# Where weight rounding, a batch's attention and its row shifts are placed at the head of an attention plus MLP kernel

## The chip, the cores and the metric

The kernel runs on one core of a Trainium2 chip. The metric is the device time of one execution in microseconds (us), as the median of several runs.

A core has five engines, each with its own list of instructions: TensorE (PE, matrix products), VectorE (DVE), ScalarE (ACT), GpSimd (POOL), and SyncE, whose queue (SPq) does nothing here but start transfers. In the traces of this case, an engine that waits holds up what stands behind in its list: in the changed kernel, a fold that TensorE needed stood on GpSimd behind an operation that waited 7.2 us for a transfer.

## The reference

```python
def reference(q, k, v, moe_w_ch1, moe_w_ch2):      # q, k, v: (8, 8, 576, 64) float32
    # attention inside chunks of 64 tokens, per batch and head
    scores = q_c @ k_c^T / sqrt(64);  attn = softmax(scores);  x = attn @ v_c   # -> (8, 576, 512)
    mixed = real(fft(fft(x, axis=1), axis=2))
    u  = x + mixed
    un = (u - mean(u)) / sqrt(var(u) + 1e-6)
    return u + relu(un @ w_ch1) @ w_ch2            # 512 -> 2048 -> 512
```

The weights arrive as 64-bit floats. The kernel turns them to 32 bits itself, with integer operations on their halves.

## The kernel before

The program is a list of steps that is written out once. Each batch has attention, a Fourier stage (products `z`, then `mix`) and an MLP (16 up steps, then down steps). The MLP of one batch is interleaved with the attention and the Fourier stage of the next. The weights come in 32 pieces of 128 x 512, and each is rounded by eight instructions on three engines. The line numbers in the traces of before (L246 and so on) are those of this code:

```python
def round_weight(i):                       # cut to its instructions
    if i < len(pieces):                    # first half of piece i
        nc.vector.tensor_scalar(wi, hi, 0x000FFFFF, None, ALU.bitwise_and)      # L244
        nc.scalar.activation(out=w, in_=wi, func=ACTF.Copy, ...)                # L245
        nc.vector.tensor_scalar(p, hi, 0x7FF00000, None, ALU.bitwise_and)       # L246
        nc.scalar.activation(out=p, in_=p, func=ACTF.Relu, ...)                 # L247, L248
    if 0 < i <= len(pieces):               # second half of piece i - 1
        nc.vector.scalar_tensor_tensor(w, lo, 2.0 ** -52, w, ALU.mult, ALU.add)             # L253
        nc.vector.scalar_tensor_tensor(p, hi, 0x80000000, p, ALU.bitwise_and, ALU.bitwise_or) # L254
        nc.gpsimd.tensor_tensor(out=w, in0=w, in1=p.bitcast(FP32), op=ALU.mult)             # L255
        ...                                # give the buffer back, start the next piece's load
```

The loop over the steps `t` of the MLPs places everything else. `conv2` combines the rounded second weight matrix into sums and differences on GpSimd (L592) and stores them for the later MLPs. It starts once rounding is through:

```python
for g in range(NG):
    for _ in mlp(g):
        t += 1
        round_next()                       # one rounding call
        if t % 2:
            round_next()                   # and a second one in every other step
        if n_w > len(pieces):              # all calls made:
            for _ in range(2):
                next(conv2, None)          # two parts of the weight combinations
        # ... other weight work cut ...
        if cur < len(sides):               # attention and Fourier stage of the next batch
            t0 = KF + 1 if cur == 0 else ready_at[cur - 1]      # KF = 16
            t1 = ready_at[cur]             # 26 for batch 1
            due = min(sizes[cur], (t - t0) * sizes[cur] // (t1 - t0))
            while done < due:
                next(sides[cur], None)
                done += 1
```

Between attention and Fourier stage stand `shift`, six small transfers that move rows by one, and `fold`, which adds and subtracts halves. For batch 1 the folds run on GpSimd.

Of the kernel before, what the change touches and what calls it, by code (L numbers as in the profile page):

```python
# [8 lines left out]
FP32 = mybir.dt.float32  # L9
U32 = mybir.dt.uint32  # L10
ACTF = mybir.ActivationFunctionType
ALU = mybir.AluOpType
# [4 lines left out]
def kernel(  # L17
# [29 lines left out]
    nc = tc.nc  # L47
# [10 lines left out]
    KF = DFF // 128  # L58
# [51 lines left out]
    tiles, first = [], []  # L110
# [22 lines left out]
    def kind(n):  # L133
        return tiles[n][0]
# [87 lines left out]
    def raw(i):  # L222
        r = raws[i]
        t = xall[:, r:r + 2, :].rearrange("p a f -> p (a f)")[:, 0:1024]
        return t.bitcast(U32).rearrange("p (f r) -> p f r", r=2)

    def load_weight(i):

        if i < len(pieces) and free and (i < N_EARLY or free[0] in RAWS[:3]):
            raws[i] = free.pop(0)  # L230
            nc.sync.dma_start(out=raw(i).rearrange("p f r -> p (f r)"), in_=pieces[i][1].bitcast(U32))

    def round_weight(i):






        if i < len(pieces):  # L240
            w, t = pieces[i][0], raw(i)
            lo, hi, wi = t[:, :, 0], t[:, :, 1], w.bitcast(U32)
            p = power[i] = three_p.tile([128, 512], U32, tag="o", name="power")
            nc.vector.tensor_scalar(wi, hi, 0x000FFFFF, None, ALU.bitwise_and)  # L244
            nc.scalar.activation(out=w, in_=wi, func=ACTF.Copy, scale=2.0 ** -20, bias=1.0)  # L245
            nc.vector.tensor_scalar(p, hi, 0x7FF00000, None, ALU.bitwise_and)  # L246
            nc.scalar.activation(out=p, in_=p, func=ACTF.Relu, scale=-1.0, bias=top[:, 0:1])  # L247
            nc.scalar.activation(out=p, in_=p, func=ACTF.Relu, scale=-8.0, bias=top[:, 1:2])  # L248
        if 0 < i <= len(pieces):
            w, t = pieces[i - 1][0], raw(i - 1)  # L250
            lo, hi = t[:, :, 0], t[:, :, 1]
            p = power.pop(i - 1)
            nc.vector.scalar_tensor_tensor(w, lo, 2.0 ** -52, w, ALU.mult, ALU.add)  # L253
            nc.vector.scalar_tensor_tensor(p, hi, 0x80000000, p, ALU.bitwise_and, ALU.bitwise_or)  # L254
            nc.gpsimd.tensor_tensor(out=w, in0=w, in1=p.bitcast(FP32), op=ALU.mult)  # L255
            r = raws.pop(i - 1)
            if i - 1 + len(RAWS) < N_EARLY or r in RAWS[:3]:
                free.append(r)
            load_weight(max(raws, default=i - 1) + 1)
# [9 lines left out]
    def att_T(n):  # L269

        a = qs.pop(n)
        pt = turn(lambda j: a[:, 2 * j:2 * j + 2, :].rearrange("p h d -> p (h d)"))
        t = one_p.tile([128, 2 * NJ, CH + 1], FP32, tag="qT", name="qT")
        low = kind(n) == LO
        nc.scalar.copy(t[:, :, CH:0:-1] if low else t[:, :, 0:CH], pt.rearrange("p j (c t) -> p (j c) t", c=2))
        if low:
            nc.gpsimd.tensor_copy(t[:, :, 0:1], t[:, :, CH:CH + 1])
        qT[n] = t
        a2 = ks.pop(n)
        pt = turn(lambda j: a2[:, 2 * j:2 * j + 2, :].rearrange("p h d -> p (h d)"))  # L280
        t = one_p.tile([128, NJ, 128], FP32, tag="kT", name="kT")
        nc.vector.tensor_copy(t, pt)
        kT[n] = t
        if first[1] <= n + 1 < NT:
            load(n + 1)
# [66 lines left out]
    def shift(b):  # L352

        lows = [xt(at[LO, b, i]) for i in range(NM)]
        r = b % 2 * CH
        rest = xt(rests[b // 2])[r:r + 1, 0:DM]
        eng = nc.gpsimd if b == 0 else nc.sync
        t = three_p.tile([128, XW], FP32, tag="y", name="first")
        for i in range(NM):
            eng.dma_start(out=t[2 * i:2 * i + 2, 0:DM], in_=lows[i][0:CH + 1:CH, 0:DM])  # L360
        eng.dma_start(out=t[2 * NM:2 * NM + 1, 0:DM], in_=rest)
        for i in range(NM):
            eng.dma_start(out=lows[i][0:CH + 1:CH, 0:DM], in_=t[2 * i + 1:2 * i + 3, 0:DM])
        eng.dma_start(out=rest, in_=t[0:1, 0:DM])
# [425 lines left out]
    with tc.manual_schedule():  # L790
        make_identity(nc, ident)
        nc.vector.memset(sign, -1.0)
        nc.vector.memset(sign[0:1, :], 1.0)
        nc.vector.memset(eps, 1e-6)
        nc.vector.memset(warm, 0.0)
        nc.vector.memset(top[:, 0:1], float((896 + 255) << 20))
        nc.vector.memset(top[:, 1:2], float(255 << 23))
        nc.scalar.preload_act_table_set("natural_log_exp_and_others")
        for n in range(3):
            load(n)  # L800
            load_v(n)
        load(3)
        load_tables()
        load_weight(0)
        load(4)
        load_weight(1)
        load_dim_tables()
        for i in range(2, len(RAWS)):
            load_weight(i)
        n_w = 0  # L810
        idle = ps_f.tile([128, 512], FP32, tag="ff", name="idle")

        def keep_warm(times):

            for _ in range(times):
                nc.tensor.matmul(out=idle[:, 0:NQ], lhsT=warm[:, 0:128], rhs=warm[:, 0:NQ], start=True, stop=True)  # L816

        def round_next():
            nonlocal n_w
            if n_w <= len(pieces):  # L820
                round_weight(n_w)
                n_w += 1

        for step, _ in enumerate(attention(0)):
            if step == 9:
                turn_tables()
            if step > 7 and step % 4 == 1:
                round_next()
            if step > 3:
                keep_warm(2)  # L830
        keep_warm(2)
        for step, _ in enumerate(fourier(0)):
            if step < 4:
                round_next()
            else:
                for s in range(2 * (step - 4), 2 * (step - 4) + 2):
                    normed(0, s)
        for s in range(G):
            keep_warm(6 if s % 2 == 0 else 0)
            turned(0, s)  # L840

        def side(b):
            yield from attention(b)
            yield from fourier(b)

        sides = [list_ for list_ in (side(b) for b in range(1, B))]
        sizes = []
        for b in range(1, B):
            n_tiles = first[b + 1] - first[b]
            sizes.append(4 * n_tiles + 4 + NM + b % 2)  # L850
        done, cur = 0, 0
        begin = [0]
        for g in range(NG):
            begin.append(begin[-1] + (KF if g < first_of[1] else 2 * HF) + (G * PARTS if g < first_of[2] else 2 * NO))
        ready_at = [begin[g] + (KF + G * PARTS - 6 if g < first_of[2] else 2 * HF + 4) for g in range(NG)]
        conv2 = iter([step for i in range(HF // 2) for step in [keep2(i)]])
        conv1 = iter([step for i in range(4) for step in [keep1(i)]])

        def chain(gens):
            for gen in gens:  # L860
                yield from gen

        conv2, conv1 = chain(conv2), chain(conv1)
        t = 0
        for g in range(NG):
            for _ in mlp(g):
                t += 1
                round_next()
                if t % 2:
                    round_next()  # L870
                if n_w > len(pieces):
                    for _ in range(2):
                        next(conv2, None)
                if t == begin[1] - 1:
                    for _ in conv2:
                        pass
                if begin[1] <= t < begin[1] + KF // 2:
                    for _ in range(3):
                        next(conv1, None)
                if t == begin[1] + KF // 2:  # L880
                    for _ in range(NS2):
                        fetch(2)
                if t == begin[1] + KF:
                    for _ in range(NS1):
                        fetch(1)
                if cur < len(sides):
                    t0 = KF + 1 if cur == 0 else ready_at[cur - 1]
                    t1 = ready_at[cur]
                    due = min(sizes[cur], (t - t0) * sizes[cur] // (t1 - t0))
                    while done < due:  # L890
                        next(sides[cur], None)
                        done += 1
                    if t >= t1:
                        for _ in sides[cur]:
                            pass
                        cur, done = cur + 1, 0
# [49 lines left out]
```

## Time and profile before

| | before |
|---|---|
| time, median (lowest to highest) | 1255.4 us (1251.8 to 1256.7) |
| span of the profiled run | 1251.5 us |
| first matmul of the first MLP | 81.3 us |
| last multiply of a weight piece starts | 160.5 us, on GpSimd |
| first score product of batch 1 starts | 166.9 us |
| first matmul of the second MLP | 272.4 us |
| from there to the end | 979.1 us |

The page gives an engine's busy share in 40 equal slices, in tenths. A PE digit under 9 is where time may be won. The stretches view, the chain of waits and the waits by engine are quoted in the prediction below. What to remember from them: PE stood 21.5 us before the first score product of batch 1 and 9.8 us before its first Fourier product. From 272 us to the end it was busy for 962 of 979 us.

### The profile page before, as it was taken

The numbers are of one execution on the slowest core, as the hardware profiler recorded it, in microseconds if no ns is written. First come the engines' busy times: TensorE is split into PE (matmuls) and PEld (weight loads), VectorE is DVE, ScalarE is ACT, GpSimd is POOL, SyncE is SP. The second block draws the span as 40 slices with busy tenths as digits, with TensorE's granted clock in tenths as the row PEclk, the third lists the DMA queues.
The fourth block names the chain that finished last, engine by engine and source line by source line (L and its number), as shares of the span: only waits on it lengthen the run. The fifth ranks groups of instructions, "written<-read, shape, count | busy, mean of one in ns | idle before, by whom it ended". The sixth has DMA issues, their size and how long they took to land.

```text
span 1251.5 us, 18517 instructions
## 1 busy us (share of the span) xinstructions
PE 1178.4 (94%) x7148; PEld 895.5 (72%) x7148; DVE 564.6 (45%) x1176; ACT 291.8 (23%) x645; POOL 308.0 (25%) x370
## 2 busy tenths in 40 slices
PE   7889666999999999999999999999999999999998
PEld 5554233444578777887788878877888788888887
DVE  4579842332334544455254535453445343423431
ACT  3347720112211321122212221122113211210310
POOL 0335445133430033102220314013402240130130
PEclk9899878999999999999999999999999999999999
DMA  9624547039524752575237524763364235445422
GB/s 196 159 93 155 166 126 208 23 102 308 155 96 144 213 147 76 158 216 158 80 140 210 170 76 135 201 179 111 125 187 129 81 122 195 155 135 182 138 70 99
DMA packets 175871, 182.11 MB, mean 146 GB/s; under 512 B 121574, under 2 KB 132327, under 8 KB 168615
## 3 DMA queue, kind: packets, MB, share of 16 engines
q1 hardware_dynamic: 173990, 180.51, 48.0%
q8 instruction: 57, 0.93, 0.3%
q10 hardware_dynamic: 1600, 0.39, 0.2%
q14 instruction: 32, 0.25, 0.1%
q0 software_dynamic: 192, 0.02, 0.0%
HBM read 156.60 MB, written 24.12 MB: 144 GB/s over the span
## 4 chain that ended last, share of the span: by engine, by line
PE 82%; DVE 9%; DMA 3%; ACT 2%; POOL 1%; SPq 1%; issue 1%; ACTq 0%; DVEq 0%; POOLq 0%
PE pb L737 18%; PE pb L690 15%; PE pa L737 14%; PE pa L690 11%; PE up L626 5%; PE pt L265 5%; PE z L442 4%; PE dn L645 3%; PE mix L485 3%; PE xp L332 2%; PE sc L294 2%; DVE power L246 1%; DMA xall<-in_moe_w_ch_dram 1%; PE idle L816 1%; DVE power L254 1%
## 5 line engine op out<-in xcount | busy, mean ns | idle before, releaser
L618 POOL TENSOR_TENSOR h<-h 128x256 f32<-128x256 f32 x64 | 56.8, 891 | 506.9 <-PE pb L690 323.4
L626 PE MATMUL up<-unT,wa 128*128 128x512 f32 x256 | 113.9, 597 | 1.8 <-ACT h L633 0.9
L737 PE MATMUL pa<-wb,h 128*128 128x256 f32 x512 | 115.6, 381 | 0.0
L737 PE MATMUL pb<-wb,h 128*128 128x256 f32 x512 | 115.1, 381 | 0.0
L690 PE MATMUL pb<-unT,wa 128*128 128x256 f32 x448 | 106.4, 380 | 8.6 <-DVE wa L699 8.6
L690 PE MATMUL pb<-wa 128*128 128x256 f32 x448 | 108.6, 385 | 1.1 <-DVE h L707 0.9
L690 PE MATMUL pa<-unT,wa 128*128 128x256 f32 x448 | 107.6, 383 | 0.0
L737 PEld LDWEIGHTS pa<-wb,h 128*128 128x128 f32 x512 | 95.8, 190 | 16.2 <-issue 3.8
L737 PEld LDWEIGHTS pb<-wb,h 128*128 128x128 f32 x512 | 95.6, 190 | 12.7
L690 PEld LDWEIGHTS pb<-unT,wa 128*128 128x128 f32 x448 | 84.5, 190 | 22.2 <-DVE wa L699 10.7
L690 PEld LDWEIGHTS pb<-wa 128*128 128x128 f32 x448 | 82.2, 190 | 16.2 <-issue 3.4
L690 PEld LDWEIGHTS pa<-unT,wa 128*128 128x128 f32 x448 | 82.5, 190 | 12.0 <-issue 1.2
L626 PEld LDWEIGHTS up<-unT,wa 128*128 128x128 f32 x256 | 47.2, 190 | 56.4 <-issue 52.0
L645 PE MATMUL dn<-wb,h 128*128 128x512 f32 x128 | 61.9, 630 | 0.0
L500 POOL TENSOR_TENSOR xall<-y,xall 128x513 f32<-128x513 f32 x16 | 27.6, 1723 | 128.9 <-DVE y L493 128.9
L737 PE MATMUL pa<-wb,yall 128*128 128x256 f32 x256 | 58.2, 381 | 0.0
L737 PE MATMUL pb<-wb,yall 128*128 128x256 f32 x256 | 57.9, 381 | 0.0
L737 PE MATMUL pb<-wb 128*128 128x256 f32 x256 | 56.6, 379 | 0.0
L690 PE MATMUL pa<-wa 128*128 128x256 f32 x224 | 53.4, 381 | 2.1 <-ACT wa L695 2.1
L697 DVE TENSOR_TENSOR wa<-pa,wa 128x256 f32<-128x256 f32 x56 | 23.8, 425 | 69.8 <-PE pa L690 69.7
L737 PEld LDWEIGHTS pa<-wb,yall 128*128 128x128 f32 x256 | 48.1, 190 | 8.6 <-issue 2.3
L737 PEld LDWEIGHTS pb<-wb 128*128 128x128 f32 x256 | 48.6, 190 | 6.6
(151 smaller groups left out, 1736.1 us busy)
## 6 DMA issues: line engine op xcount, KB each, us to landing
wb<-s SPq DMA_DIRECT2D x56, 1024.0 KB
wa<-s SPq DMA_DIRECT2D x196, 256.0 KB
xall<-in_moe_w_ch_dram SPq DMA_DIRECT2D x32, 512.0 KB
v<-in_v_dram SPq DMA_DIRECT2D x142, 64.0 KB
s<-yall SPq DMA_DIRECT2D x24, 256.0 KB
s<-wb SPq DMA_DIRECT2D x20, 256.0 KB
q<-in_q_dram SPq DMA_DIRECT2D x34, 128.0 KB
k<-in_k_dram SPq DMA_DIRECT2D x34, 128.0 KB
```

The costliest lines, as they stand in the source:

```text
L265: nc.tensor.transpose(pt[:, j, :], src(j), ident)
L294: nc.tensor.matmul(out=sc[t0:t0 + CH, e, j * CH:(j + 1) * CH], lhsT=a[r0:r0 + D, 2 * j + c, 0:CH], rhs=b[r0:r0 + D, j, t0:t0 + CH], start= ...
L332: nc.tensor.matmul(out=xp[t0:t0 + CH, e, j * D:(j + 1) * D], lhsT=a[r0:r0 + CH, j, t0:t0 + CH], rhs=b[r0:r0 + CH, c, j, :], start=True, st ...
L442: nc.tensor.matmul(out=z[:, 0:NQ], lhsT=pm[p, fold_, half], rhs=tk[p, i, fold_, :], start=(i == 0), stop=(i == NM), skip_group_check=(T == 2),
L485: nc.tensor.matmul(out=o[:, cols], lhsT=zt[:, T], rhs=tab, start=(T == 0), stop=(T == 3), skip_group_check=True,)
L500: eng.tensor_tensor(out=x[:, 0:w], in0=y[:, 0:w], in1=x[:, 0:w], op=ALU.add)
L618: nc.gpsimd.tensor_tensor(out=h1[:, m, hi], in0=h1[:, m, lo], in1=h1[:, m, hi], op=ALU.subtract)
L626: nc.tensor.matmul(out=up, lhsT=w1[:, kk, m * 128:(m + 1) * 128], rhs=unT[:, kk], start=(kk == 0), stop=(kk == KD - 1),)
L645: nc.tensor.matmul(out=dn, lhsT=h1[:, m, s * 128:(s + 1) * 128], rhs=w2[:, m, :], start=(m == 0), stop=(m == KF - 1),)
L690: nc.tensor.matmul(out=dst, lhsT=w[:, kk, r], rhs=rhs[o][:, kk], start=(o in (0, 2) and kk == 0), stop=(kk == 1), skip_group_check=True,)
L697: nc.vector.tensor_tensor(out=b, in0=dst, in1=a, op=ALU.add)
L737: nc.tensor.matmul(out=dst, lhsT=lhs[:, m], rhs=w[:, m], start=(o in (0, 2) and m == 0), stop=(m == HF - 1), skip_group_check=True,)
```

## The change

The intent is to fill these waits. The multiply L255 leaves GpSimd. Batch 1's attention is spread over 18 steps of the first MLP instead of 9. The key copies of batches 0 and 1 go to ScalarE and the row shifts of batch 1 to GpSimd's queue. Two smaller edits move rounding calls.

```diff
-            nc.gpsimd.tensor_tensor(out=w, in0=w, in1=p.bitcast(FP32), op=ALU.mult)
+            nc.vector.tensor_tensor(out=w, in0=w, in1=p.bitcast(FP32), op=ALU.mult)
@@ att_T: key copy
-        nc.vector.tensor_copy(t, pt)
+        if n < first[2]:
+            nc.scalar.copy(t, pt)
+        else:
+            nc.vector.tensor_copy(t, pt)
@@ shift
-        eng = nc.gpsimd if b == 0 else nc.sync
+        eng = nc.gpsimd if b < 2 else nc.sync
@@ first Fourier stage
-            if step < 4:
+            if step < 3:
                 round_next()
-            else:
+            elif step > 3:
                 ... normalise ...
@@ loop over the MLP steps
-                if t % 2:
+                if t % 2 == 0:
                     round_next()
@@
-                    t0 = KF + 1 if cur == 0 else ready_at[cur - 1]
+                    t0 = KF // 2 if cur == 0 else ready_at[cur - 1]
```

## The prediction

> **What bounds the kernel now.** I read the page first, for where TensorE (PE) is not full.
>
> ```profile
> PE   7889666999999999999999999999999999999998
> DVE  4579842332334544455254535453445343423431
> PEclk9899878999999999999999999999999999999999
> ```
>
> A digit is a tenth of a slice of 31.3 us. PE shows 9 (90% or more) from the eighth slice on, so the shortfall lies early. Next, the chain of waits: from 272.47 us, the second MLP's first matmul, it is almost only matmuls, so those 979 us are PE's own work, and the change leaves their program order alone. Everything must come from before 272. The stretches view splits the first MLP (us, busy time per engine with instruction counts, granted clock, DMA):
>
> ```profile
> 81.00:145.00 64.00, 62.78 (x150) 27.98 (x151) 57.86 (x85) 47.19 (x76) 30.65 (x20) 1.00 0.45 147
> 145.00:167.00 22.00, 0.45 (x8) 0.21 (x7) 14.50 (x20) 10.23 (x17) 13.03 (x11) 0.60 0.36 97
> 167.00:204.00 37.00, 34.70 (x354) 19.78 (x354) 16.40 (x30) 6.87 (x12) 13.80 (x17) 0.96 0.67 181
> 204.00:214.00 10.00, 0.22 (x1) 0.22 (x2) 0.07 (x1) 0.00 (x0) 4.51 (x9) 0.68 0.88 253
> 214.00:222.00 8.00, 8.00 (x12) 3.34 (x13) 0.19 (x1) 0.46 (x2) 4.10 (x5) 0.55 0.71 236
> ```
>
> Two holes: 145 to 167 and 204 to 214, the second followed by 8 us at about half clock. The waits by engine name their ends:
>
> ```profile
> PE sc L294 <- POOL qT L277: 21.5, 1, 21.5
> PE z L442 <- POOL pm L388: 9.8, 1, 9.8
> ```
>
> The first hole: up to 145 us PE ran ahead (16 up steps of 3.44 us, two down steps), then met the first score product of batch 1. That product needs copies of its queries and keys, which stand on ScalarE (ACT), VectorE (DVE) and GpSimd (POOL) behind the rounding of all 32 weight pieces; the last piece leaves POOL at 161.7, and four POOL subtractions of the first weight combination come before the query copy. The second: the Fourier product waits for a fold on POOL, which waits for row shifts and for stores on SyncE's backed-up queue. Why rounding lags, in order of time:
>
> ```profile
> 100.39 1.42 DVE power L246
> 101.81 0.60 DVE wa L253
> 102.41 0.64 DVE power L254
> ...
> 151.83 3.71 DMA xall<-in_moe_w_ch_dram
> 155.56 1.03 DVE wb L244
> 156.59 0.34 DVE power L246
> ```
>
> A piece costs DVE 0.34 + 1.42 + 0.60 + 0.60 = 2.96 us to about 127 us. L246 takes 0.34 us alone, but 1.42 whenever POOL's multiply (L255, median 1.386 us) runs beside it. After 127 us three buffers are left and two pieces take 6.2 us, half of that a transfer.
>
> **What the Trainium skill says.** "SBUF — State Buffer", section "SBUF: two separate sides": DVE and GpSimd share a port pair as an exclusive lock for a whole instruction. The trace agrees: 1.42 against 0.34 us. "GPSIMD Engine Reference", section "Engine selection": elementwise two-input work is about twice as slow on GpSimd. Agrees: 1.39 us against 0.60 to 0.68 for DVE's two-input L253. "TensorE: Matmul & The Clock Gate", section "Why this matters for your kernels": no PE gaps over about 3 us, or the clock halves. Agrees: 0.55 granted after the 9.8 us hole. "DMA: Bandwidth & Descriptors", section "Issuing engines are not separate DMA queues": another issuing engine saves only sequencer time. Here this is the point: SyncE issued without a break from 190.3 to 204 us at about 0.6 us each, with the shift in the middle at 195.9.
>
> **The change part by part.**
>
> Multiply on DVE: per piece DVE loses the 1.08 us blockage and gains a two-input instruction, which I put at L253's 0.60. New cost 0.34 + 0.34 + 3 x 0.60 = 2.48 us, 0.48 less. ACT needs about 1.9 us per piece (three instructions; starts at 85.50 and 87.39) plus 0.5 per up step. With 1.5 pieces per step DVE needs 3.72 us a step, ACT 3.35, PE 3.44: nearly level. POOL is free, so the query copy no longer stands behind anything.
>
> Head of the program: one rounding call fewer in the first Fourier stage. There the ACT chain of the last call (65.76 to 67.7) stood before the copy of the mix at 67.66, whose data needed only the evict that ended at 64.85 and a 0.5 us matmul. Worth about 2 us, and key copies on ACT take 0.56 us from in front of the first row shift (key copy 31.23, x write 31.79). I take 2.5 us for both. The call itself moves into the first MLP.
>
> Attention of batch 1 now starts after up step 8 instead of 16 and runs 23 parts over 18 steps instead of 9. Before, 2 parts were done when rounding ended; now 12. On PE the ten extra parts are 2.5 tiles of 2.55 us (queries and keys 0.87, scores 0.62, weights turned 0.44, values 0.62), 6.4 us that fall into the old hole. On DVE the same parts cost: four score groups of 2.5 us plus about 0.7 of waiting for the exponential, two value writes of 0.68, 14 us in all, now between pieces. So DVE from 81 to the last piece: 26 first halves x 0.68 + 27 second halves x 1.80 = 66.3, plus 14, plus about 4 us at the start (ACT is held by the first evict until PE ends an up step at 85.0, then the second) = 165.4 us. That is 4 us later than 161.7: the freed DVE time is spent on attention. I walked the steps on all four engines with these durations; PE waits about 6 us at its first score product (113 to 119), keeps DVE's pace, and ends its 19th step with the two attention parts behind it near 169 to 170 us.
>
> From there PE has 13 down steps x 3.44 = 44.7, two attention parts 1.1, Fourier and mix 15.1, turned activations 1.8, first parts of batch 2 4.0: 66.7 us. Before, the same reckoning from 167 gives 79.3 us of work against 105.5 elapsed, so 26 us of waits and slow clock.
>
> How much of this wait stays? The shift goes to POOL's own queue and ends, after the batch 1 value write near 159, by about 166 to 168 (three issues, a landing, three issues; batch 0's took 10 us). It is then off the path. But batch 1's last fold still stands on POOL behind the second weight combination, which waits for stores of the first: issue near 175, landing 5 us later as at 173.2 to 178.3, then 3 x 1.27 of subtractions and 2.4 of fold, so near 186.5. PE reaches its first Fourier product near 180.5: still a 6 us hole, plus about 4 us at half clock (before: 9.8 and 4). The end (mix, statistics, normalise, turn) keeps about 5 us of waits, a little less because the first mix is one step earlier. Sum: 169.5 + 66.7 + 6 + 4 + 5 = 251 for the start of the second MLP, against 272.5, and 248.5 with the 2.5 us of the head. **Gain 24 us**, and 1255 - 24 = 1231; I round to 1230, since nothing is counted for steps that run ahead.
>
> **The rivals.**
> (a) Lockstep. With attention among the pieces the four in-order engines wait for each other every step: ACT's up evict waits for PE, PE for ACT's query copy, DVE for PE's scores. For it: DVE and ACT are within 11% of each other per step, and a stalled PE falls to half clock. Against: PE has slack to 169 us either way. If it costs 1 us in each of the ten steps with attention, 1240.
> (b) Both holes close. If POOL's earlier start on combinations (free since about 167) and the free SyncE queue put the fold ahead of PE, the 6 + 4 us vanish: 1220. Against: the store wait occurred three times in the trace (20.5 us in total) and the order between fold and combination is unchanged.
> (c) Transfers stay the bound of rounding. 3.5 us to land against 3.1 us of DVE work between freeing and reuse in the three-buffer ring; with attention in between it is about 3.9, so transfers should be hidden. Were they not, the last piece would come at most 3 us later: 1233.
> (d) The gain is given back after 272. PE is at 9 tenths in every slice and keeps its order there, so no: time won before goes through to the end.
>
> **Range and chances.** Rivals (a) and (b) set the spread: 1219 to 1241. The 2% line is 1229.9, on my centre. Faster by over 2% 0.48, within 2% 0.51, slower 0.01: no part adds PE work, and PE now idles over 30 us before 272.
>
> **What would show it.** L246 at about 0.42 us throughout, the multiply on DVE at 0.6 to 0.7, GpSimd nearly idle from 81 to 155. The last piece at 160 to 168. The 21.5 us wait of PE for the query copy gone, in its place one of about 6 us near 115 and short ones to 160. A wait of the first Fourier product for the fold of 3 to 8 us, now near 182. The first mix copy near 65.5 instead of 67.66. First matmul of the second MLP near 248 instead of 272.5, and 979 us from there to the end. I am wrong in the mechanism if the last piece is past 172 or before 155, if the Fourier product waits for nothing, or if the stretch after the second MLP's start changes by over 3 us.

## The result, and the profile after

The changed kernel takes 1237.5 us in the median (1234.4 to 1239.9, four runs) against 1255.4 (four runs). The ratio is 0.986, with a 95% interval of 0.983 to 0.989. A ratio here is the mean time of one kernel's runs over that of the other's in the same rounds, so it is not quite the ratio of the medians. The gain is 17.9 us where 24 to 25 was expected. The profiled run was the fastest of the four, and its span (1232.6 us) is 18.9 us shorter than that of the profiled run before, so the two traces differ by 1 us more than the medians.

The same rows of the changed kernel's page (busy tenths in 40 slices of 30.8 us, granted clock):

```profile
PE   7798987999999999999999999999999999999998
DVE  3678860523244535455345444552545343523421
PEclk9898998999999999999999999999999999999999
```

The run of three 6s in PE has gone. What remains is an 8 in the fourth slice and an 8 and a 7 in the sixth and seventh. The stretches of the changed kernel, cut at its own waits (length, busy us and count of PE, weight loads, DVE, ACT and POOL, then clock, DMA share, GB/s):

```profile
78.00:142.00 64.00, 56.70 (x236) 27.03 (x237) 54.33 (x106) 47.81 (x79) 0.57 (x2) 0.95 0.55 156
142.00:165.00 23.00, 18.61 (x113) 9.41 (x111) 20.87 (x42) 16.99 (x28) 1.60 (x3) 0.93 0.70 174
165.00:184.00 19.00, 18.51 (x144) 9.21 (x142) 9.61 (x14) 2.50 (x5) 11.42 (x16) 1.00 0.60 142
184.00:192.00 8.00, 0.00 (x0) 0.00 (x0) 0.00 (x0) 0.00 (x0) 5.74 (x7) 0.68 0.72 230
192.00:200.00 8.00, 7.80 (x15) 3.57 (x16) 0.19 (x1) 0.46 (x2) 7.03 (x8) 0.68 0.25 88
```

The 22 us in which PE stood are filled: from 142 to 165 it works 18.6 of 23 us. DVE is now the fullest engine there (20.9 of 23). A stretch without any PE work remains from 184 to 192, the old second hole; the granted clock is 0.68 in it and in the 8 us after it. The waits of PE by engine (total us, times, longest us) name both that are left:

```profile
PE z L445 <- POOL pm L391: 8.7, 1, 8.7
PE sc L297 <- ACT kT L283: 6.0, 1, 6.0
```

Rounding in the changed kernel, from the chain of waits (start, us, engine, tile, line). It answers the three lines of 100 to 103 us in the prediction:

```profile
101.11 0.61 DVE power L254
...
101.74 0.69 DVE wa L255
102.43 0.34 DVE wa L244
102.77 0.34 DVE power L246
103.11 0.60 DVE wa L253
```

L246 takes 0.34 us instead of 1.42, with GpSimd idle. The multiply costs DVE 0.69 us. A piece is 0.34 + 0.34 + 0.60 + 0.63 + 0.69 = 2.60 us from start to start, against 2.96 before.

The second MLP starts at 253.6 us, and from there to the end it is 979.0 us as before. So only what lies before the second MLP changed: the first MLP starts at 78.3 us instead of 81.3, and takes 175.3 instead of 191.1.

The remaining hole in the chain of waits of the changed kernel, in order of time:

```profile
167.25 1.29 POOL yall L595
...
177.34 8.58 DMA s<-yall
...
186.05 1.26 POOL yall L595
...
187.39 2.48 POOL yall L595 x2
...
190.08 1.27 POOL sum L380
...
191.42 0.74 POOL pm L391
...
192.20 2.59 PE z L445 x4
```

Read from the bottom: the Fourier product waits for the fold (`pm`). The fold's sum stands on GpSimd behind three operations of the second weight combination (186.05 and 187.39). Those overwrite `yall` and so wait, 7.2 us, until the first combination's stores (`s<-yall`) have read it.

### The profile page after: what moved, and what is told of

It reads as the page before. It is cut to its first block, busy times and chain, and to the rows that moved or that the text cites. A ratio compares the mean times of both kernels' runs of the same rounds, so it can differ in the third digit from the quotient of the medians.

```text
span 1232.6 us, 18509 instructions
## 1 busy us (share of the span) xinstructions
PE 1176.6 (95%) x7148; PEld 893.8 (73%) x7148; DVE 560.2 (45%) x1199; ACT 296.0 (24%) x654; POOL 266.1 (22%) x344
## 4 chain that ended last, share of the span: by engine, by line
PE 82%; DVE 8%; DMA 3%; ACT 3%; POOL 2%; issue 1%; SPq 0%; POOLq 0%; ACTq 0%; DVEq 0%
PE pb L740 18%; PE pb L693 15%; PE pa L740 14%; PE pa L693 11%; PE up L629 6%; PE pt L265 4%; PE z L445 4%; PE mix L488 3%; PE xp L335 2%; PE dn L648 2%; PE sc L297 2%; PE idle L819 1%; PE z L455 1%; DVE ex L308 1%; DMA first<-xall 1%
## 5 line engine op out<-in xcount | busy, mean ns | idle before, releaser
L629 PE MATMUL up<-unT,wa 128*128 128x512 f32 x256 | 117.4, 607 | 0.9 <-DVE unT L537 0.9
L693 PEld LDWEIGHTS pb<-unT,wa 128*128 128x128 f32 x448 | 84.5, 190 | 22.2 <-DVE wa L702 10.7
## 6 DMA issues: line engine op xcount, KB each, us to landing
wa<-s SPq DMA_DIRECT2D x196, 256.0 KB
s<-yall SPq DMA_DIRECT2D x24, 256.0 KB
s<-wb SPq DMA_DIRECT2D x20, 256.0 KB
```

The source lines that it names most:

```text
L629: nc.tensor.matmul(out=up, lhsT=w1[:, kk, m * 128:(m + 1) * 128], rhs=unT[:, kk], start=(kk == 0), stop=(kk == KD - 1),)
L693: nc.tensor.matmul(out=dst, lhsT=w[:, kk, r], rhs=rhs[o][:, kk], start=(o in (0, 2) and kk == 0), stop=(kk == 1), skip_group_check=True,)
```

## The experiments

Three theories were on the table. Theory A: DVE's rounding chain sets when PE may go on, and the hole at the Fourier product is the fold queued behind the second combination. Rival B: the hole is the round trip of the row shift. Rival C: transfers, or the lockstep of four in-order engines, set the pace of rounding by now. All kernels gave correct results. All times are medians of four runs, ratios are to the kernel before in the same rounds, and the changed kernel is 0.986. The experiments ran on three chips, on which the kernel before took 1254.9 to 1257.1 us, so a difference of 2 us between two medians shows nothing.

### The multiply back on GpSimd (u_mult)

```diff
-            nc.vector.tensor_tensor(out=w, in0=w, in1=p.bitcast(FP32), op=ALU.mult)
+            nc.gpsimd.tensor_tensor(out=w, in0=w, in1=p.bitcast(FP32), op=ALU.mult)
```

> The changed kernel with the multiply of the weight pieces back on GpSimd, all else kept. Theory A (VectorE's rounding chain sets when PE may go on, and the port shared with GpSimd slows it): L246 goes back to 1.4-1.5 us, a piece costs VectorE 2.96 instead of 2.60 us, the last piece ends 7 to 10 us later than 168 us, second MLP starts near 262 instead of 253.6, time 1245 us (1242 to 1248). Rival C (transfers or the lockstep with PE and ScalarE set the pace of rounding by now): the slack takes it up, at most 2 us, 1237 to 1239.

Measured: 1239.2 us, ratio 0.987 (0.984 to 0.990). The second MLP starts at 256.5 us, 3 us later. Theory A's size is refuted, and the time is the one that rival C gave. L246 did go back to 1.4 us up to 134 us. Later the attention's instructions stand between the pieces and L246 takes 0.42 us in the records again. DVE then runs out of pieces instead, as its waits in this run show (us, times, longest):

```profile
DVE wb L244 <- DMA xall<-in_moe_w_ch_dram: 6.1, 5, 2.1
```

In the changed kernel the same wait is 1.4 us in total. DVE's last rounding instruction (L254) ends at 169.0 us, as the last multiply does in the changed kernel (169.1): without the multiply DVE has less to do for a piece, and late in the phase this pays for the early stretching and the waits. On GpSimd the last three multiplies stand behind the row shift, which waits 5.0 us for its own transfer. They run from 170.3 to 174.0, the first combination follows them, and the first Fourier product starts at 193.8 us instead of 192.2.

### The multiply alone, on the kernel before (a_mult)

```diff
-            nc.gpsimd.tensor_tensor(out=w, in0=w, in1=p.bitcast(FP32), op=ALU.mult)
+            nc.vector.tensor_tensor(out=w, in0=w, in1=p.bitcast(FP32), op=ALU.mult)
```

> The kernel before with only the multiply moved to VectorE. Theory A: the last piece ends 5 to 7 us before 161.7 and the query copy no longer queues behind multiplies and follows at once, so the 21.5 us wait shrinks to 13 to 16 us; the second wait stays; 1246 to 1250. Theory C1 (transfers in the three-buffer ring hide it): 1252 to 1256.

Measured: 1247.1 us, ratio 0.994 (0.992 to 0.996), as theory A expected. The last multiply starts at 156.7 us (it ends 4.3 us before 161.7, a little less than expected), and PE's first wait is 13.6 us instead of 21.5. The second grew to 11.7. So the same edit is worth about 8 us by itself and, inside the whole change, 1 to 2 us, which lies within the spread. It and the spread attention fill the same hole.

### Batch 1's attention from step 17 again (u_spread)

```diff
-                    t0 = KF // 2 if cur == 0 else ready_at[cur - 1]
+                    t0 = KF + 1 if cur == 0 else ready_at[cur - 1]
```

> The changed kernel with batch 1's attention started at step 17 again, all else kept. Theory A: rounding ends 12 to 14 us earlier (154 to 156 us), but PE idles until then and has the attention after it: second MLP starts at 258 to 262, time 1243 us (1240 to 1247). Rival C (lockstep between the four engines during the spread attention costs what the spread gains): 1237 us or less.

Measured: 1243.3 us, ratio 0.990 (0.986 to 0.993), as theory A expected. The last multiply starts at 156.9 us, PE waits 13.3 us for the keys of the first score product, and the second MLP starts at 263.5, some 2 us later than expected. Spreading the attention is worth some 5 us here, although it puts off the start of the last multiply by 10.

### Batch 1's row shift back on SyncE (u_shift)

```diff
-        eng = nc.gpsimd if b < 2 else nc.sync
+        eng = nc.gpsimd if b == 0 else nc.sync
```

> The changed kernel with batch 1's row shift back on SyncE's queue. Theory A (the hole before the Fourier product is the last fold queued on GpSimd behind the second combination, which waits for the first one's stores; these are issued after the output store at 175.65 us whoever issues the shift): the Fourier wait stays 7 to 10 us, time within 2 us of the changed kernel. Rival B (the shift's round trip sets the hole): the wait changes by 4 us or more, and the time with it; 1242 us or more if SyncE's queue is the worse place.

Measured: 1236.0 us, ratio 0.984 (0.982 to 0.987). The Fourier wait is 8.7 us, unchanged. In the profiled run, the slowest of the four, the second MLP starts at 256.0 us, 2.5 us later than in the changed kernel; the times don't show that. Rival B falls: the queue of the shift is worth nothing measurable here.

### The key copies back on VectorE (u_key)

```diff
-        if n < first[2]:
-            nc.scalar.copy(t, pt)
-        else:
-            nc.vector.tensor_copy(t, pt)
+        nc.vector.tensor_copy(t, pt)
```

> The changed kernel with the key copies of batches 0 and 1 back on VectorE. Theory A (VectorE is the engine that paces rounding and attention together): four copies of 0.6 to 0.7 us more on it before the last piece, and one in front of the first row shift; second MLP starts 2 to 4 us later (256 to 258), time 1240 us. Rival (ScalarE is loaded nearly as much, so either engine will do): 1236 to 1238.

Measured: 1238.5 us, ratio 0.985 (0.983 to 0.987). No difference is shown. The profiled run has its second MLP at 260.2 us, but it was the slowest of the four runs (1241.0, the fastest 1235.0), so this one trace doesn't decide for theory A.

### Batch 1's folds and second add on VectorE (n_fold2)

```diff
-        eng = nc.vector if b == 0 else nc.gpsimd                 # fold
+        eng = nc.vector if b < 2 else nc.gpsimd
+        sm = nc.vector if b == 1 else nc.gpsimd                  # used for the small copies and the clear
@@ normalisation add
-                eng = nc.gpsimd if kind(n) == HI else nc.vector
+                eng = nc.gpsimd if kind(n) == HI and b != 1 else nc.vector
```

> The changed kernel with batch 1's folds, the small copies and the clear beside them, and its second normalisation add on VectorE instead of GpSimd, so that nothing of batch 1's Fourier stage queues behind the weight combinations. Theory A: the wait of the Fourier product for the fold (8.7 us, and some 3 us at slow clock) goes; second MLP starts 9 to 13 us earlier, 241 to 245 us; time 1226 us (1223 to 1230). Rival B (the shift sets the hole): the wait stays, since the shift is as before, and time 1235 to 1238.

Measured: 1226.1 us, ratio 0.977 (0.974 to 0.980), as theory A expected. PE has no wait at all between 165 and 200 us, and the second MLP starts at 245.4. The shift was as in the changed kernel. So the last hole is the order on GpSimd's list.

### The rounding calls where they were (u_round)

```diff
-            if step < 3:
+            if step < 4:
                 round_next()
-            elif step > 3:
+            else:
@@
-                if t % 2 == 0:
+                if t % 2:
                     round_next()
```

> The changed kernel with the rounding call of the first Fourier stage and the old odd/even placing back. Theory A (ScalarE's three instructions of that call stand before the first mix copy): that copy starts at 67 to 68 us instead of 65.16, the first MLP 2 to 3 us later than 78.34; one call less afterwards gives about 1 us back; time 1238 to 1240. Rival (the call only moves and costs the same anywhere): 1237 within 1 us.

Measured: 1226.2 us, ratio 0.975 (0.974 to 0.977), 11 us faster than the changed kernel by the medians and 13 by the ratios. Both theories missed this by far, although the head did as theory A says: the first mix copy starts at 68.25 instead of 65.16 us, the first MLP at 81.57 instead of 78.34. The chain of waits of this run at the place of the hole:

```profile
182.18 3.63 PE dn L648 x8
185.81 1.72 PE z L445 x6
187.53 3.63 PE dn L648 x8
```

The hole has gone. The program says why. With the old placing the last rounding call is made in step 17, with the new one in step 18, and the weight combinations start when it has been made. The issues on SyncE's queue show what one step does, first in the changed kernel, then in this run (start, length, line, what, count):

```profile
170.23 0.39 SPq L167 DMA_DIRECT2D q<-in_q_dram  x1
170.73 0.52 SPq L167 DMA_DIRECT2D k<-in_k_dram  x1
171.33 3.30 SPq L177 DMA_DIRECT2D v<-in_v_dram  x4
175.65 0.62 SPq L557 DMA_DIRECT2D out_dram<-o  x1
176.32 0.46 SPq L599 DMA_DIRECT2D s<-wb  x1
176.89 3.13 SPq L599 DMA_DIRECT2D s<-yall  x3
```

```profile
163.00 0.60 SPq L599 DMA_DIRECT2D s<-wb  x1
170.78 1.55 SPq L599 DMA_DIRECT2D s<-yall  x3
172.38 0.99 SPq L599 DMA_DIRECT2D s<-wb  x2
173.47 0.49 SPq L599 DMA_DIRECT2D s<-yall  x1
...
180.25 0.62 SPq L557 DMA_DIRECT2D out_dram<-o  x1
```

In the changed kernel the stores of `yall` stand behind batch 2's loads and behind the output store, and leave at 176.9 us. Here they are ahead of them and leave at 170.8, as soon as GpSimd has the first results. The second combination can then start at 174.1 us, after a wait of 0.85 us, instead of 186.05 after one of 7.2. Of these 12.0 us the later issue is 6.1. The rest is the landing: in the changed kernel the store that is waited for takes 8.6 us from issue to landing (177.3 to 185.9). Why so long is open; the loads and the output store issued just before it are the obvious suspects, but no run moves the stores alone. This became theory D: the step at which the combinations start is the cause. Its rival E: the old rounding itself paces the phase better. The next two runs cross the two.

### The new rounding, the combinations from step 17 (n_early)

```diff
-                if n_w > len(pieces):
+                if t > KF:
                     for _ in range(2):
                         next(conv2, None)
```

> The changed kernel with the weight combinations started at step 17, as in the kernel before and in the run with the old rounding, instead of step 18; the new rounding stays. Theory D (the old rounding won 11 us only because it ends at step 17, so the first combination's stores are put on SyncE's queue at step 19, ahead of batch 2's first loads, of the values of its rest tile and of the output store at step 20, and the second combination no longer waits): the 8.7 us wait of the Fourier product goes, the first MLP still starts near 78.3 us, second MLP near 242, time 1222 to 1226. Rival E (the old rounding itself paces the phase better): the wait stays, 1235 to 1238.

Measured: 1229.5 us, ratio 0.979 (0.977 to 0.981). The wait is down to 0.7 us, and the first MLP starts at 78.6:

```profile
PE z L445 <- POOL pm L391: 0.7, 1, 0.7
```

In the profiled run (1225.2 us) the second MLP starts at 244.5, 2 us later than expected. The three other runs took 1229 to 1231 us. What makes them longer no trace shows. Theory D holds in mechanism, and its time was missed by 3 us.

### The old rounding, the combinations held to step 18 (u_round_late)

```diff
-                if n_w > len(pieces):
+                if t > KF + 1:
                     for _ in range(2):
                         next(conv2, None)
```

(on top of the edit of u_round)

> The changed kernel with the old rounding, but the combinations held to step 18. Theory D: the wait of 7 to 10 us at the Fourier product comes back, time 1236 to 1241. Rival E: it stays away, 1226.

Measured: 1237.0 us, ratio 0.986 (0.984 to 0.987). The wait is back:

```profile
PE z L445 <- POOL pm L391: 8.7, 1, 8.7
```

The four cells of the cross:

| | combinations from step 17 | from step 18 |
|---|---|---|
| old rounding | 1226.2 us | 1237.0 us |
| new rounding | 1229.5 us | 1237.5 us (the changed kernel) |

One step of the combinations is worth 8 to 11 us (9 to 13 by the ratios). The rounding's new placing is worth nothing by itself, or costs 3 us (4.5 by the ratios) where the combinations start early. Theory D is settled as to the step, and rival E falls. That the step acts through the order on SyncE's queue is read from the traces; no run changes this order by itself.

### Four weight buffers to the end (n_ring), and with the multiply on GpSimd (u_mult_ring)

```diff
     N_EARLY = 20
+    LATE = RAWS[:3] + RAWS[4:]             # and LATE for RAWS[:3] where buffers are reused
```

> The changed kernel with four buffers for weight pieces kept to the end instead of three after piece 20. Rival C1 (landing transfers limit rounding late in the phase): VectorE's 1.4 us of waits for them go, and up to 4 us on the chain at 144.6; the last piece ends 2 to 4 us earlier, time 1234 to 1236. Theory A1 (VectorE's own work is the limit): less than 1 us, 1236 to 1238.

> The multiply back on GpSimd and four buffers to the end. The multiply alone moved back cost only 2 us, and its trace shows VectorE waiting 6.1 us for transfers in the late part, where each piece costs it 2.2 us. Theory C1 (there transfers hid what the multiply costs or saves): with the fourth buffer these 6 us go, second MLP starts 4 to 6 us before 256.5, time 1233 to 1236, no worse than the multiply on VectorE with the same buffers. Rival (the shared port costs it anyway): 1238 to 1240 as before.

Measured: 1235.3 us, ratio 0.983 (0.981 to 0.985) and 1237.6 us, ratio 0.985 (0.983 to 0.987). In both, the table of waits no longer lists DVE as waiting for a weight transfer. With the multiply on VectorE the last multiply starts 1 us earlier, between what the two theories expected, and the gain lies within the spread. With it on GpSimd the second MLP starts 2.6 us earlier than without the fourth buffer (253.9 against 256.5), about half of what theory C1 asked for. So late transfers are most of what the multiply on GpSimd costs in the traces: the second MLP's start differs by 3.0 us between the two places with three buffers (256.5 against 253.6) and by 0.3 with four (253.9 against 253.6). In the times it is about 2 us with either buffer count, and in both pairs the runs overlap.

### What points to a better version, together (n_best3)

The early combinations, the folds and the add on VectorE, and four buffers.

> The changed kernel with the combinations from step 17, batch 1's folds and second add on VectorE, and four buffers for weight pieces to the end. If each removes a wait of its own: 1219 to 1223. If folds on VectorE and early combinations remove the same wait (theory A with D) and the fourth buffer is worth little: 1222 to 1226, as the early combinations alone.

Measured: 1225.1 us, ratio 0.976 (0.975 to 0.977). That is the second outcome foreseen: the two cures remove the same wait and don't add. It beats both kernels by a clear margin (12 us under the changed one). Against u_round (0.975) and n_fold2 (0.977) it is no different.

## Why the prediction was right or wrong

**What bounds the kernel, and where the gain can come from:** right. From the second MLP's start to the end it is 979.0 us against 979.1. Rival (d), that the gain is given back there, is excluded.

**The multiply on DVE:** the mechanism was right, a size off. L246 stays at 0.41 to 0.43 us in the records throughout (0.34 from start to start). The multiply was put at "L253's 0.60" and adds 0.72, so a piece is 2.60 us and not 2.48. Over 27 pieces that is 3.2 us. The timeline shows where the 0.12 lie. The next instruction starts 0.61 us after the multiply, as after L253. But L255 reads what L254 writes, and it starts only when L254's record has ended (101.03 + 0.68, then 101.74), where L254 itself starts 0.07 us before the end of L253's record.

**The head:** right in this trace. 2.96 us earlier (81.30 to 78.34) for 2.5. The first mix copy starts at 65.16 us for 65.5. Other kept traces with the same head start the first MLP at 78.6 to 80.5 us (n_early, n_best3), those with the old rounding at 81.3 to 81.6, so the gain is 1 to 3 us. But it was booked as a gain without its price: moving the call also moved the end of rounding from step 17 to 18, and with it the start of the combinations. The prediction's rival (b) says "the order between fold and combination is unchanged". That sentence is the step that failed. On GpSimd three combinations, twelve operations, stood before the first fold of batch 1 in the kernel before; one stands there in the changed kernel. The combinations moved back one step while the folds moved forward, and their stores fell behind other issues on SyncE's queue. The cross of four runs shows 8 to 11 us for that step. The hole itself was forecast, as a fixed part of the kernel. That the two smallest edits of the change keep it open was not seen.

**The walk to the last piece:** the shape was right, too short. The first wait of PE came as foretold (6.0 us, ending at 116.3 us). The sum was to run 84 us (81.3 to 165.4). It ran from 78.34 to 169.08, when the last multiply ended: 90.7 us. Of these 6.6 us too many the multiply's size explains 3.2, and the last multiply itself 1.1, as it took 1.77 us beside the first GpSimd subtraction instead of 0.69. Waits for transfers are 1.4 us, which rival (c) had called hidden. Two more errors nearly cancel, which was luck. Four score groups were booked before the last piece, but only three stand there (at 117.5, 136.3 and 151.2 us; the fourth at 169.0): three of 3.16 and two value writes of 0.60 are 10.7 us for 14. And DVE's other waits for ScalarE and PE are 7.1 us in the table of waits for the 4 booked, so some 3 us can be said for rival (a). About 1 us is left unexplained. The last piece, at 169.1 us, is just past the 160 to 168 that were named.

**The hole:** 6 us and 4 at slow clock were foreseen, and 3 to 8 us named as the sign. Measured were 8.7 us and about 3 (2.59 us for four Fourier products and 4.8 for the down step after them; at full clock these take about 1.1 and 3.44). The store in question left at 177.3 us instead of the expected 172.5 (175 less the head's 2.5), and took 8.6 us to land instead of 5.

**The sum:** second MLP at 253.6 us for 248.5, 5.1 us late. The rest of the difference between 1230 and 1237.5 us is that the profiled run is 3 us under the median.

**The parts, by undoing each:** the spread attention is worth some 5 us, the multiply 1 to 2 at most, the queue of the shift and the place of the key copies nothing that shows, and the rounding calls cost 11 or more. The prediction called the shift's place in SyncE's queue "the point". It had argued from SyncE's issuing without a break in the trace before. But that queue was late because of what stood in it, and in the new order the shift was not what the fold waited for.

## What to carry to other kernels

When a schedule starts one chain of work at the end of another, a small edit that moves this end by one step can reorder the queues of several engines behind it. Look up there what now stands in front of what, before the edit is booked as a gain. Two edits that fill the same hole don't add: test each alone and each undone. And where an engine off the critical path has small work that the critical path waits for, keep that work off any list that also waits for stores.

## What the Trainium skill lacked or had wrong

- "SBUF — State Buffer", section "SBUF: two separate sides": the exclusive lock agrees (0.34 against 1.42 us for L246). What the page has no figure for is how little of it may be left in the time: with other work between the pieces, giving the multiply back to GpSimd cost 1 to 2 us of 1237.
- "SBUF — State Buffer", same section: that a VectorE operation with two SBUF inputs and a GpSimd operation that reads SBUF block each other agrees with the last multiply, 1.77 us instead of 0.69 beside a GpSimd subtraction.
- No page that was read has a figure for what a VectorE instruction loses when it reads what the one before it wrote: L255 starts 0.71 us after L254, and L254, which doesn't depend on L253, 0.60 us after that.
- "DMA: Bandwidth & Descriptors", section "Issuing engines are not separate DMA queues": it agrees that another issuing engine saves little (1236.0 against 1237.5 us). No page that was read says what the order within one issuing queue can cost: with stores issued 6 us later behind loads and an output store (176.9 against 170.8 us), and one of them 8.6 us from landing, a hole of 8.7 us came back.
